# Nine units for twelve, states on the whole array and the first tap on ScalarE, in a kernel of decay attention and gated convolution

## The chip, the cores and the metric

The kernel runs on one core of a Trainium2 chip. The metric is device time in microseconds (us), as a median of runs. The five engines are TensorE (PE in the profile; PEld is its weight load), VectorE (DVE), ScalarE (ACT), GpSimd (POOL) and SyncE (SP), which here only issues transfers.

## The reference

Four batches, eight heads, 768 steps, head width 48. Each head keeps a 48x48 complex state that decays per key channel; its real part, read by the query, is the output of the step. The outputs of all heads, side by side (384 channels), go through a causal convolution of five taps whose sigmoid gates a projection, and a second projection follows.

```python
scale = np.minimum(mag, 0.999) / (mag + 1e-06)        # mag = |a|
a_re_n, a_im_n = a_re * scale, a_im * scale
for t in range(S):
    S_re, S_im = ar * S_re - ai * S_im + k[t] (x) v[t], ar * S_im + ai * S_re
    y[t] = q[t] . S_re
gate = 1 / (1 + np.exp(-sum(conv_w[k] * xp[:, k:k + S])))   # x = y of all heads, 5 taps
out = (gate * (x @ w_val)) @ w_out
```

## The kernel before

The loop over steps is turned into chunks of 128 steps. The running product of the decays is kept as a level (a log magnitude) and an angle, summed along time. Keys are divided and queries multiplied by that product (as cosine and sine, so 96 numbers for a head), after which the work of a chunk is: scores of keys against queries, a triangular mask, the masked scores against v, and the queries against the state that all earlier chunks left.

A **unit** is one tuple (batch, first head, heads, half, halves): the heads of one half (384 steps) of a batch that are prepared together. The kernel before has twelve: batch 0 is cut into 2, 2 and 4 heads for each half, the others are 8 heads wide. For each unit a chain of small steps runs on ScalarE and VectorE: logarithm, exponential, arctangent, the sums along time, two small matmuls that carry sums across partitions (`j`, `l`), sine and cosine, and at the end the scaled keys `kx` (second step of `q`) and scaled queries `qx` (second step of `r`). ScalarE reads a function from one of three table sets, and `act()` issues a table load (line 136) wherever the next function's set is not the one loaded.

From there two ways lead on. TensorE transposes `kx` and `qx` (`T`, three matmuls for a head; ScalarE copies the result out, `U`); and `kx` is stored to DRAM and read back in another layout (`K` then `N`, tiles `kd` and `kn`), because the state update needs steps on the partitions. Per chunk and group of up to two head pairs follow: scores `s`, mask `M` (VectorE), state update `t` into the one bank `S_ps` and its copy `u` (ScalarE), output `y` into `y_ps` and its copy `v` (ScalarE). Before the change `t` issues two matmuls of 64 weight columns for a head (and each is two instructions on the engine, since the data are float32); `kn` has 32 padding columns that GpSimd zeroes.

Finished outputs go by transfers on GpSimd's queue (`X`) into `xT`, 384 channels on the partitions. VectorE runs the taps of the convolution (`C`, `D`: one TENSOR_SCALAR, four SCALAR_TENSOR_TENSOR for a third of the channels), ScalarE the sigmoid (`G`), TensorE the value product (`P`, six instructions), VectorE the gating (`Z`), TensorE the output product (`O`, six), ScalarE the copy (`Q`), GpSimd the store (`W`). Four PSUM buffers named `mm` serve `j`, `l`, `T`, `P` and `O` in turn.

The order of all this is the string `ORDER`: each letter advances one stream by a step. `turn()` ties each instruction of PE, DVE and ACT to the one before it on its engine, so these three run in the order of the string. Transfers are not tied (`PIN_SP` is False).

## Time and profile before

| | before |
|---|---|
| median of 3 runs | 343.71 us (341.5 to 344.56) |
| profiled execution, first to last instruction | 343.3 us |
| PE busy | 279.2 us, 3219 matmuls |
| DVE busy | 256.9 us, 394 instructions |
| ACT busy | 252.8 us, 480 instructions |
| table loads on ACT | 34 |

The profiled execution has no other time of its own than its span, which lies 0.4 us under the median. A busy PE is not a PE at its peak, since matmuls overlap. The windows below give for a stretch of the span how long each engine was busy, how many instructions it ran, and the TensorE clock that was granted.

### The profile page before, as it was taken

The page shows a single profiled execution, that of the slowest core. Times are in us where ns is not written, and L with a number is a line of the kernel's source. Part 1 is how long each engine was busy: PE and PEld are TensorE (multiplying, and loading weights), DVE is VectorE, ACT ScalarE, POOL GpSimd, SP SyncE. Part 2 cuts the span into 40 slices and gives each one's busy share as a digit, 9 for nine tenths or more (in the row PEclk, how much of TensorE's full clock was granted, in tenths as well). Part 3 has the DMA queues.
Part 4 walks back from the last instruction along what each step waited for, and adds up shares of the span by engine and source line. Part 5 has one row for each costly group of instructions (what it writes and reads, how often), then busy time and mean ns, then how long its engine had stood idle before and what let it go on. Part 6 is the DMA issues. An engine that isn't in the chain of part 4 may idle for free.

```text
span 343.3 us, 8085 instructions
## 1 busy us (share of the span) xinstructions
PE 279.2 (81%) x3219; PEld 213.4 (62%) x3219; DVE 256.9 (75%) x394; ACT 252.8 (74%) x480; POOL 61.6 (18%) x141
## 2 busy tenths in 40 slices
...
GB/s 146 195 340 156 199 212 171 2 208 174 135 270 228 47 240 342 218 304 236 80 243 244 187 267 257 238 135 29 60 250 194 164 193 20 38 35 69 69 73 2
DMA packets 87497, 57.23 MB, mean 167 GB/s; under 512 B 43791, under 2 KB 82974, under 8 KB 86686
## 3 DMA queue, kind: packets, MB, share of 16 engines
...
q8 instruction: 27, 0.44, 0.6%
...
## 4 chain that ended last, share of the span: by engine, by line
PE 42%; ACT 14%; DVE 13%; DMA 13%; issue 11%; POOL 3%; SPq 1%; POOLq 0%; DVEq 0%; ACTq 0%
PE mm L513 10%; DMA kn<-kd 8%; PE mm L714 6%; PE y_ps L617 4%; PE sc_ps L542 4%; PE S_ps L580 4%; ACT L136 4%; PE mm L348 4%; DMA kd<-kx 3%; DVE kx L463 3%; PE mm L707 3%; PE y_ps L627 2%; PE y_ps L622 2%; ACT tmp L138 2%; ACT qx L138 2%
## 5 line engine op out<-in xcount | busy, mean ns | idle before, releaser
L676 DVE SCALAR_TENSOR_TENSOR z<-xT,cw_sb,z 128x384 f32<-128x384 f32 x96 | 55.3, 614 | 0.9
L148 POOL DMA_DIRECT2D xT<-y_sb x80 | 40.9, 517 | 77.4 <-ACT y_sb L141 69.4
L714 PE MATMUL mm<-w_sb,z 128*128 128x384 f32 x144 | 48.7, 489 | 2.7 <-DVE z L731 2.3
L707 PE MATMUL mm<-xT,w_sb 128*128 128x384 f32 x144 | 50.5, 499 | 0.0
L136 ACT ACT_TABLE_LOAD x34 | 43.6, 1283 | 1.4 <-PEq L940 0.8
L542 PE MATMUL sc_ps<-qT,kT 96*64 96x128 f32 x192 | 38.9, 300 | 3.2 <-ACT qT L141 2.5
L138 ACT ACTIVATE main<-main 128x1152 f32<-128x1152 f32 (+2 forms) x48 | 40.3, 842 | 1.4 <-DVE main L432 0.8
L558 DVE TENSOR_TENSOR sm<-sc_ps,mask 128x384 f32<-128x384 f32 (+1 forms) x54 | 27.1, 510 | 19.1 <-PE y_ps L627 11.4
L513 PE MATMUL mm<-ident,kx 128*96 128x128 f32 x192 | 30.1, 304 | 12.8 <-DVE kx L463 12.2
L714 PEld LDWEIGHTS mm<-w_sb,z 128*128 128x128 f32 x144 | 26.9, 190 | 21.2 <-DVE z L731 3.1
L543 PE MATMUL sc_ps<-qT,kT 96*64 96x128 f32 x192 | 38.9, 300 | 0.0
L707 PEld LDWEIGHTS mm<-xT,w_sb 128*128 128x128 f32 x144 | 27.2, 195 | 17.1 <-issue 0.6
L580 PE MATMUL S_ps<-v_in,kn 128*64 128x48 f32 x640 | 29.2, 236 | 5.8 <-DMA kn<-kd 4.3
L513 PEld LDWEIGHTS mm<-ident,kx 128*96 128x96 f32 x192 | 23.1, 140 | 16.3 <-issue 7.4
L141 ACT COPY qT<-mm 96x384 f32<-96x384 f32 x64 | 27.7, 485 | 6.5 <-PE mm L513 6.5
L141 ACT COPY y_sb<-y_ps 112x256 f32<-112x256 f32 (+1 forms) x54 | 18.3, 356 | 18.7 <-PE y_ps L627 18.6
L580 PEld LDWEIGHTS S_ps<-v_in,kn 128*64 128x64 f32 x640 | 25.1, 150 | 11.0 <-issue 6.6
L513 PE MATMUL mm<-ident,qx 128*96 128x128 f32 x192 | 28.6, 290 | 1.8 <-DVE qx L463 1.8
L141 ACT COPY kT<-mm 96x384 f32<-96x384 f32 x64 | 27.5, 483 | 3.3 <-PE mm L513 2.7
L141 ACT COPY ot<-mm 128x384 f32<-128x384 f32 x24 | 11.3, 472 | 23.7 <-PE mm L714 20.3
L544 PE MATMUL sc_ps<-qT,kT 96*64 96x64 f32 x192 | 28.4, 232 | 0.0
L547 PE MATMUL sc_ps<-qT,kT 96*64 96x64 f32 x192 | 28.2, 231 | 0.0
...
## 6 DMA issues: line engine op xcount, KB each, us to landing
...
```

What stands on the lines that cost most here:

```text
L136: turn("act", nc.scalar.preload_act_table_set(sets[0]))
L138: return turn("act", nc.scalar.activation(*args, **kw))
L141: return turn("act", nc.scalar.copy(out, in_))
L148: ins = (nc.gpsimd if pool else nc.sync).dma_start(**kw)
L513: pe(nc.tensor.transpose(pt[:C2, j, :], src[:, j, f, h, :], ident))
L542: pe(nc.tensor.matmul(lo[:, :C], part(u, 0, ha, n, 0, HC), part(u, 1, ha, n), start=True, stop=True))
L543: pe(nc.tensor.matmul(hi[:, 0::2], part(u, 0, hb, n, 0, HC), qb, start=True, stop=True))
L544: pe(nc.tensor.matmul(lo[:, C:], part(u, 0, hb, n, HC, C), part(u, 1, hb, n, HC, C), start=True, stop=True))
L580: pe(nc.tensor.matmul(S_ps[b][c:c + 64, head(u, h) * D:(head(u, h) + 1) * D], kn[:, at:at + 64], v_b[b][:, head(u, h), n], start=(i == fir ...
L676: dve(nc.vector.scalar_tensor_tensor(out=z, in0=xT[:, c, EXT + t0 - t:EXT + t0 - t + n], scalar=cw_sb[:, TAPS - 1 - t, c:c + 1], in1=z, op ...
L707: pe(nc.tensor.matmul(pv[:, :n], wv_sb[:, ci, c * P:(c + 1) * P], xT[:, ci, EXT + t0:EXT + t0 + n], start=(ci == 0), stop=(ci == NT - 1),))
L714: pe(nc.tensor.matmul(po[:, :DM], z[:, ci, m:m + P], wo_sb[:, ci, :], start=(ci == 0), stop=(ci == NT - 1)))
```

## The change

- **Units**: batch 0 is cut into 2 heads, 6 heads (first half) and 8 heads (second half): nine units for twelve. `groups` is made so that head pairs keep their places.
- **Tiles**: `main` (level and angle in one tile, three buffers) becomes `lv` and `an`, two buffers each; the negative exponential of `p_exp` goes into a tile `em` of its own, which shares two buffers with `tmp`.
- **Convolution**: `CONVS` runs over 768 steps at once for batches 0 to 2 and in two halves for batch 3. The first tap runs on ScalarE (`TAP0 = 'act'`).
- **States**: `t` issues one matmul with 96 weight columns for a head instead of two with 64; the padding of `kn` and its memset go, and the columns of `S_ps` are laid out so that `u` reads one run.
- **Outputs**: `y_ps` becomes one slot in a bank, instead of two slots in a bank.
- **Order**: a new string. The `pool()` helper changes nothing while `PIN_SP` is False.

```diff
-UNITS = ((0, 0, 2, 0, 1), (0, 1, 2, 0, 1), (0, 2, 4, 0, 1), (0, 0, 2, 1, 1), (0, 1, 2, 1, 1), (0, 2, 4, 1, 1), (1, 0, 8, 0, 1), (1, 0, 8, 1, 1), (2, 0, 8, 0, 1), (2, 0, 8, 1, 1), (3, 0, 8, 0, 1), (3, 0, 8, 1, 1))
+UNITS = ((0, 0, 2, 0, 1), (0, 1, 6, 0, 1), (0, 0, 8, 1, 1), (1, 0, 8, 0, 1), (1, 0, 8, 1, 1), (2, 0, 8, 0, 1), (2, 0, 8, 1, 1), (3, 0, 8, 0, 1), (3, 0, 8, 1, 1))
 PIECES = ((0, 0, 384), (0, 384, 384), (1, 0, 384), (1, 384, 384), (2, 0, 384), (2, 384, 384), (3, 0, 384), (3, 384, 384))
-CONVS = ((0, 0, 384), (0, 384, 384), (1, 0, 384), (1, 384, 384), (2, 0, 384), (2, 384, 384), (3, 0, 384), (3, 384, 384))
+CONVS = ((0, 0, 768), (1, 0, 768), (2, 0, 768), (3, 0, 384), (3, 384, 384))
 GROUPWISE = True
-BUFS = {'in': 4, 'v': 2, 'kn': 2, 'xT': 2, 'z': 3, 'main': 3, 'tmp': 1, 'qx': 2, 'kx': 1, 'kT': 6, 'S': 1, 'S_sb': 3, 'S_cr': 4, 'y_sb': 3, 'sm': 2, 'ot': 2, 'mm': 4}
-YSLOTS = 2
+BUFS = {'in': 4, 'v': 2, 'kn': 2, 'xT': 2, 'z': 2, 'lv': 2, 'an': 2, 'tmp': 2, 'qx': 2, 'kx': 1, 'kT': 6, 'S': 1, 'S_sb': 3, 'S_cr': 4, 'y_sb': 3, 'sm': 2, 'ot': 2, 'mm': 4, 'y': 1}
...
+TAP0 = 'act'
 ORDER = (
-    "AAVaaaabbcVcedhhVjfkgkciicleAmAdAnhhojoAkknLoLoLfpgipiqlAamrpqAaArTpKbTUTwcAwwTwcUeUUwwsfwwgsMMsdqry"
-    "AhivhqjNMTraTakKUbUAkcicnAewwfAlTmNTgdwUtUoshuiohijwlsmktawyapMbsukcqtctpAeyquuftvMuTKvgnrTUiTArUATU"
-    "iwUlTATUTUmtNwTyyMuXvwvyaXvawXUbUwsXcscetMdMsdhwuohwojtyuktvMyukwnyvohohvwjXkwpkpqXqpAprTKrfATUgATUA"
-    "CTUCUDnCsqsCNqoMTMoCTKCUDAsUCyDCPaMCDvaNCDbGtrPcZArdiAiAluGTmTUtZUtuhsuGthsjyckyPupevpMMvsZaXyqyvMXA"
-    "vqaykvTKfXTbTTXUUgOUUnriOcArQNcWiTlUeATQUTWATmUUfssMgstdyMiuMvtohyiuhlvojmykOvVXkpQqpXqAnWaaDTKCTDUC"
-    "TUDTUCPUDCDCoDboPDcDDdPDrhGAGZAGZZrONpcAqTQTTUWTUeATUTUTUThUTqpjsastaMKMskuyUtUTMUTbUTuTvTftktryuunt"
-    "gyuvtNUrUTUTUsuAvscXAMTAMTcsiiyXUUMlUUTmvTTteTdyuyhvohttUUjUUTkvTuTXusoktsMTMspXyUyMUqUTUTuOnCAqvvpy"
-    "OUCKUDQCvDfXsCDsQMaTMXsCUyaCDyCvNMTDvTWUCTUybUWPvVCXCgGPGGZciXPZdirlZAomOAAoDDOCQDWCDpOCDDQqpWPDcACD"
-    "tQPCuWDDGrtGPGuZTZtUZtuhTuTrUTUTUTTUhATUjqTtassaMKMsAkyUyUMUvbTuTUTvTkTtrnyNUUTUTUesuAvsXMfTMTsgyXUy"
-    "UUMUTivTvTicltcmyueUtUtUsvusXuMftMsgyydMXiTThUTUiTUhlUvTvmTUTuyoCDjUCUODvoCXDCOQDXCDCGOkGQCWskpsWMCs"
-    "nMyqpyMPQqvWvyoCKTZVTCUTUTrUPUvorXPGZTNZXTUTUOUOpDQDpWqOQDWCTDTUCTUsDUDsMDsGMyQDTWMTUDTUTqUTUtvTutyu"
-    "DKtCvtuyCuCtUrTUTGsGUsMUvsMuXrtyNuyvXTvTMUTUEyUEvTETXUTUTUTUsUsMtMXsuttuyutMvyCDyvCuDTCTUTDUTUTCTUDP"
-    "UUCDGCGCsvZXsMMsCyXCyMvCyGvPvXPZXPZOZDDODQWDDODGDQDWDPCDQCWCPCCZPGZGOZOQWOQWPQWPZZOOQWOQWQW"
+    "AaaabaLwwwwwwAbwwVAcccefgiilmceAAAdhhjdphhkkLjkkqAfgiinproAoqrKnooaalmppNwwbcdcqrTTAATqraKVthehUafuj"
+    "bktUcTTUgkceUUisMsiuslnfMdtgwoioThNyilmpUTUmAATUhqMLTTvUUTUTuUpyvTTtqUTsMyutssrTTpuMUUvryUMUtwsvyTpT"
+    "AuAaMwvabtTwssUuwcyMvjAkceAktKNyMvTUUUuryvtTfTgwqnUAAAATTiyUUssTTTXMutivoyoqusUTdtUUUlTuUUtTMTXXTXvy"
+    "rmXutMaKhThvyaUTUbUsvwMjpXkcUqyvsMcsMkUpTuUNyvTTynVUUvTTeXrXwwXUUsstwTMTTMTsXfgywooutvMyutqCvCyCDDCu"
+    "DtUUTUUATUTTTUUUsUvuwTsTPUMysTMCCdthGvuDhUPUDjGArZtyZTaMTTvyaiUUKkNUvTTiUluknssUbcmpCTTPMUyCtCswdMMu"
+    "tvTooyAqAPAuCAXUvyqGZOTcQZTteOpUTAUutTrrUTQOvhUTuUXfsgiMisaabyUUvlKsXTTcMyhmjXUcMvykNkWQXpXPPZVvetpn"
+    "oToXWqZOUTODDDDutUTUCTCutXQTCUTUsTDsUPCutMDDdsyGCUPMGZDTDWhWQDAZqhvryuvOQGPZrfWWtugAOOUjMQUaakQATUTA"
+    "yTUbUTTUTUiUvcissWlMyTkncsUTTUmMvtuKpNATMUqUyvWoPTZTTyUUAeoTTvTsMtufsyMsqKNgtivypuAitUOUTMUTUXrXTvyd"
+    "QuthUhjvTuUPUkUssMsyvMlknooWmZPZpyvOQprOQMyvVtuqTUTUTTUUtTrTTUUUTTUTTTUsMUsyTTMqrXXutvuyvtustUUUUuMX"
+    "XTTTXCXKyTUTUssUMMWvyNTsTvyMDUUUDCUtvyuTTTvCUCTTUUstUUsMWTCsMyMutTDTTCCGXDXUTvyutXUTUvyutXUUUssMsMPP"
+    "vyMPPZDvyXCOvuXCCyGZPQGZZZWODvXXCDDDPZDGDCQWDDDPDZPCOQWOQOOWQQOECCGZPCDPGDDPZCCOCCCCCCCWQOWQGWOZPQDD"
+    "GZGZOWQOOWEEWQWQQWW"
 )
...
-    groups = [[range(r, min(r + 2, g // 2)) for r in range(0, g // 2, 2)] for b, h0, g, f0, nf in units]
+    groups = [
+        [range(max(r, h0) - h0, min(r + 2, h0 + g // 2) - h0) for r in range(h0 - h0 % 2, h0 + g // 2, 2)]
+        for b, h0, g, f0, nf in units
+    ]
...
+    def bank(u, rs):
+        b, h0, g, f0, nf = units[u]
+        return b, (h0 + rs[0]) // 2 % BUFS["S"]
+
     firsts = {}
     for i, (u, n, rs) in enumerate(chunks):
-        firsts.setdefault(units[u][0], i)
+        firsts.setdefault(bank(u, rs), i)
 
...
-        flat = tl[u]["kn", f] = sb.tile([C, HN * g * C2 + 32], F32, name="kn", bufs=BUFS["kn"])
-        nc.gpsimd.memset(flat[:, HN * g * C2:], 0.0)
-        kn = flat[:, :HN * g * C2].rearrange("i (n h c) -> i n h c", n=HN, h=g)
+        flat = tl[u]["kn", f] = sb.tile([C, HN * g * C2], F32, name="kn", bufs=BUFS["kn"])
+        kn = flat.rearrange("i (n h c) -> i n h c", n=HN, h=g)
...
-    y_ps = ps.tile([P, YSLOTS * 256], F32, name="y_ps")
+    y_ps = [ps.tile([P, 512], F32, name=f"y_ps{i}") for i in range(BUFS["y"])]
     sc_ps = [ps.tile([P, 512], F32, name=f"sc_ps{i}") for i in range(2)]
-    for t in [y_ps] + sc_ps:
+    for t in y_ps + sc_ps:
         dve(nc.vector.memset(t, 0.0))
...
+    def rate(u, nm, tag):
+        b, h0, g, f0, nf = units[u]
+        tl[u][nm] = sb.tile([P, JH, nf, g * D], F32, name=nm, tag=tag, bufs=BUFS[tag])
+        return views(u, nm)
...
-        tmp = tl[u]["tmp"] = sb.tile([P, nf * g * D * JH], F32, name="tmp", bufs=BUFS["tmp"])
+        tf, tj = rate(u, "tmp", "tmp")
...
+        ef, ej = rate(u, "em", "tmp")
+        act(ef, lf, AF.Exp, scale=-0.5, accum_out=over[:, 0, u:u + 1], sets=[LE])
+        yield
+        act(lf, lf, AF.Exp, scale=0.5, accum_out=over[:, 1, u:u + 1], sets=[LE])
...
-            if i == firsts[b]:
-                S_ps[b] = ps.tile([P, 512], F32, name="S_ps", bufs=BUFS["S"])
+            if i == firsts[bank(u, rs)]:
+                S_ps[bank(u, rs)] = ps.tile([P, 512], F32, name="S_ps", bufs=BUFS["S"])
             kn = tl[u]["kn", n // HN]
             for r in rs:
-                for h in (r, r + g // 2):
-                    for c in range(0, P, 64):
-                        at = ((n % HN) * g + h) * C2 + c
-                        pe(nc.tensor.matmul(
-                            S_ps[b][c:c + 64, head(u, h) * D:(head(u, h) + 1) * D], kn[:, at:at + 64],
-                            v_b[b][:, head(u, h), n],
-                            start=(i == firsts[b] and r == rs[0] and h == r), stop=(n == NCH - 2),
-                            skip_group_check=True,
-                        ))
+                for w in range(2):
+                    h = r + w * (g // 2)
+                    at = ((n % HN) * g + h) * C2
+                    pe(nc.tensor.matmul(
+                        S_ps[bank(u, rs)][:C2, (2 * (h0 + r) + w) * D:(2 * (h0 + r) + w + 1) * D], kn[:, at:at + C2],
+                        v_b[b][:, head(u, h), n],
+                        start=(i == firsts[bank(u, rs)] and r == rs[0] and w == 0), stop=(n == NCH - 2),
+                        skip_group_check=True,
+                    ))
...
-            t = sb.tile([C2, 2, len(rs) * D], F32, name=nm, bufs=BUFS[nm])
-            act_copy(t, S_ps[b][:C2, :H * D].rearrange("c (w x) -> c w x", w=2)[
-                :, :, (h0 + rs[0]) * D:(h0 + rs[-1] + 1) * D
-            ])
+            t = sb.tile([C2, 2 * len(rs) * D], F32, name=nm, bufs=BUFS[nm])
+            act_copy(t, S_ps[bank(u, rs)][:C2, 2 * (h0 + rs[0]) * D:2 * (h0 + rs[-1] + 1) * D])
...
-        return y_ps[:, (i % YSLOTS) * 256:(i % YSLOTS + 1) * 256]
+        return y_ps[i % BUFS["y"]][:, :256]
...
-        dve(nc.vector.tensor_scalar_mul(z, x0, w0))
+        if TAP0 == "act":
+            act(z, x0, AF.Copy, scale=w0)
+        else:
+            dve(nc.vector.tensor_scalar_mul(z, x0, w0))
```

## Rows read from the trace of the kernel before

**Rows 1.** The page: span, and busy time of each engine

```profile
span 343.3 us, 8085 instructions
...
PE 279.2 (81%) x3219; PEld 213.4 (62%) x3219; DVE 256.9 (75%) x394; ACT 252.8 (74%) x480; POOL 61.6 (18%) x141
```

**Rows 2.** Windows: length; busy us of PE, PEld, DVE, ACT, POOL; clock, DMA share

```profile
0.00:140.00 140.00, 91.23 (x829) 69.47 (x830) 110.69 (x188) 117.61 (x218) 18.43 (x55) 0.90 0.75 192
140.00:333.00 193.00, 187.99 (x2392) 143.91 (x2390) 146.26 (x207) 135.21 (x263) 42.60 (x85) 1.00 0.62 156
...
60.00:70.00 10.00, 6.70 (x116) 5.92 (x112) 6.13 (x9) 6.09 (x13) 2.38 (x6) 0.81 0.05 14
70.00:80.00 10.00, 7.67 (x52) 6.27 (x54) 9.69 (x21) 9.31 (x20) 0.67 (x2) 0.53 0.78 226
110.00:120.00 10.00, 9.00 (x110) 6.85 (x110) 5.36 (x7) 5.90 (x9) 1.91 (x5) 0.83 0.24 55
```

**Rows 3.** The chain of the whole span, in order of time: start, us, what

```profile
44.98 1.21 DVE kx L463
...
49.82 0.98 PE mm L513 x9
...
52.11 5.48 DMA kn<-kd
...
105.01 5.47 DMA kn<-kd
...
237.24 5.80 PE mm L714 x18
...
267.38 2.48 DVE kx L463
...
275.79 8.10 DMA kn<-kd
```

**Rows 4.** Timeline of PE, 283 to 293 us: start, us, line, out<-in

```profile
284.31 0.29 PE L542 MATMUL sc_ps<-qT,kT 96*64 96x128 f32 x1
...
284.66 0.28 PE L542 MATMUL sc_ps<-qT,kT 96*64 96x128 f32 x1
...
285.00 1.09 PE L580 MATMUL S_ps<-v_in,kn 128*64 128x48 f32 x32
285.92 0.61 PE L617 MATMUL y_ps<-qT,S_cr 96*48 96x128 f32 x8
286.36 0.40 PE L622 MATMUL y_ps<-sm,v_in 128*48 128x64 f32 x8
286.58 0.39 PE L627 MATMUL y_ps<-sm,v_lo 128*48 128x64 f32 x8
```

**Rows 5.** Timeline of PE, 181 to 196 us

```profile
183.49 0.39 PE L627 MATMUL y_ps<-sm,v_lo 128*48 128x64 f32 x8
183.81 6.07 PE L707 MATMUL mm<-xT,w_sb 128*128 128x384 f32 x18
```

**Rows 6.** Timeline of PE, 327 to 333 us

```profile
326.62 5.65 PE L714 MATMUL mm<-w_sb,z 128*128 128x384 f32 x17
```

**Rows 7.** Groups by line and shape: count, busy us, mean ns, idle before

```profile
L676 DVE SCALAR_TENSOR_TENSOR z<-xT,cw_sb,z 128x384 f32<-128x384 f32 x96 | 55.3, 614 | 0.9
...
L136 ACT ACT_TABLE_LOAD x34 | 43.6, 1283 | 1.4 <-PEq L940 0.8
...
L138 ACT ACTIVATE main<-main 128x1152 f32<-128x1152 f32 x24 | 28.0, 1166 | 0.3
...
L138 ACT ACTIVATE z<-z 128x384 f32<-128x384 f32 x24 | 11.6, 524 | 4.6 <-DVE z L676 4.5
...
L673 DVE TENSOR_SCALAR z<-xT,cw_sb 128x384 f32<-128x384 f32 x24 | 9.7, 417 | 2.9 <-DMA xT<-y_sb 2.9
...
L461 DVE TENSOR_TENSOR main<-main,k_in 128x1152 f32<-128x1152 f32 x6 | 8.1, 1353 | 1.7 <-ACT main L138 1.7
...
L461 DVE TENSOR_TENSOR main<-main,k_in 128x288 f32<-128x288 f32 x4 | 1.8, 452 | 0.1
```

More of the change, by code (lines that the diff above doesn't have):

```diff
@@ L132, in dve, with pool @@
         return turn("dve", ins)
+    def pool(ins):
+        return turn("pool", ins) if PIN_SP else ins
     def act(*args, sets=(), **kw):
@@ L148, in dma @@
         ins = (nc.gpsimd if pool else nc.sync).dma_start(**kw)
-        return turn("sp", ins) if PIN_SP and not pool else ins
+        return turn("pool" if pool else "sp", ins) if PIN_SP else ins
     def load(u, nm):
@@ L357, in p_ln @@
     def p_ln(u):
-        b, h0, g, f0, nf = units[u]
-        tl[u]["main"] = sb.tile([P, 2, JH, nf, g * D], F32, name="main", bufs=BUFS["main"])
-        main, mf, mj = views(u)
-        act(mj[:, 0], jm(tl[u]["ar"]), AF.Ln, sets=[LE])
+        lf, lj = rate(u, "lv", "lv")
+        act(lj, jm(tl[u]["ar"]), AF.Ln, sets=[LE])
         yield
-        act(mf[:, 1], mf[:, 0], AF.Exp, scale=-1.0, accum_out=over[:, 2, u:u + 1], sets=[LE])
+        af, aj = rate(u, "an", "an")
+        act(af, lf, AF.Exp, scale=-1.0, accum_out=over[:, 2, u:u + 1], sets=[LE])
         yield
     def p_tan(u):
-        main, mf, mj = views(u)
-        dve(nc.vector.tensor_tensor(out=mj[:, 1], in0=mj[:, 1], in1=jm(tl[u]["ai"]), op=ALU.mult))
+        af, aj = views(u, "an")
+        dve(nc.vector.tensor_tensor(out=aj, in0=aj, in1=jm(tl[u]["ai"]), op=ALU.mult))
         yield
     def p_sec(u):
-        b, h0, g, f0, nf = units[u]
-        main, mf, mj = views(u)
-        tmp = tl[u]["tmp"] = sb.tile([P, nf * g * D * JH], F32, name="tmp", bufs=BUFS["tmp"])
-        act(tmp, mf[:, 1], AF.Square)
+        tf, tj = rate(u, "tmp", "tmp")
+        act(tf, views(u, "an")[0], AF.Square)
         yield
-        act(tmp, tmp, AF.Ln, bias=1.0, sets=[LE])
+        act(tf, tf, AF.Ln, bias=1.0, sets=[LE])
         yield
     def p_arc(u):
-        main, mf, mj = views(u)
-        act(mf[:, 1], mf[:, 1], AF.Arctan, sets=[TRIG, SIG])
+        af, aj = views(u, "an")
+        act(af, af, AF.Arctan, sets=[TRIG, SIG])
         yield
     def p_mag(u):
-        main, mf, mj = views(u)
+        lf, lj = views(u, "lv")
         dve(nc.vector.scalar_tensor_tensor(
-            out=mf[:, 0], in0=mf[:, 0], scalar=2.0, in1=tl[u]["tmp"], op0=ALU.mult, op1=ALU.add
+            out=lf, in0=lf, scalar=2.0, in1=views(u, "tmp")[0], op0=ALU.mult, op1=ALU.add
         ))
@@ L392, in p_inv @@
     def p_inv(u):
-        main, mf, mj = views(u)
-        act(tl[u]["tmp"], mf[:, 0], AF.Exp, bias=b_inv, scale=-0.5, sets=[LE])
+        act(views(u, "tmp")[0], views(u, "lv")[0], AF.Exp, bias=b_inv, scale=-0.5, sets=[LE])
         yield
     def p_min(u):
-        main, mf, mj = views(u)
+        lf, lj = views(u, "lv")
         dve(nc.vector.scalar_tensor_tensor(
-            out=mf[:, 0], in0=mf[:, 0], scalar=2.0 * math.log(0.999), in1=tl[u]["tmp"],
+            out=lf, in0=lf, scalar=2.0 * math.log(0.999), in1=views(u, "tmp")[0],
             op0=ALU.min, op1=ALU.subtract,
```

53 lines of the change are left out of this document (26 added, 27 removed).

## The prediction

> **What bounds the kernel now.** I read the page first: three engines are busy for three quarters of the span or more and none for all of it [rows 1]. Such shares are averages over unlike stages, so I cut the span into windows and looked for the place where the engine with no pause changes. It lies near 140 us [rows 2]. Before it ScalarE is busy for 117.6 of 140 us and VectorE for 110.7, while TensorE shows 91 us of busy time that is mostly single matmuls waiting one by one. After it TensorE is busy for 188 of 193 us at full clock, and ScalarE for 135. So the time is a sum of two stages: a front that ends when ScalarE has done 117.6 us of its own work, and a rest that lasts as long as TensorE's remaining work. The last matmul ends at 326.62 + 5.65 = 332.3 us [rows 6], and the last copy, the last store and the closing of the program take 343.3 - 332.3 = 11.0 us more.
>
> To see whether the rest is work or waiting, I priced TensorE's steps by their steady rate, from the start of one run of matmuls to the start of the next. Three transposes of a head (`T`): 9 in 0.98 us, so 0.327 us. A `P` or `O` of six: 18 in 5.80 us, so 1.935 [rows 3]. Scores of a head pair: 284.66 - 284.31 = 0.35; I take 0.34. States of a head pair, eight instructions: (285.92 - 285.00) / 4 = 0.23. Outputs of a pair: 0.44 / 2 = 0.22 for the carried part and 0.22 for the two masked parts together [rows 4]. An offset (`j`, `l`) of 8 heads is two instructions of 384 columns, 0.65. One price more: the eight masked matmuls at 183.49 should take 0.22 us, as in rows 4, but the value product behind them begins 0.32 us later [rows 5]. Going from matmuls that use part of the columns to ones that use all of them costs 0.10 us; I charge the same for the way back.
>
> The order string shows how many steps lie behind 140 us (the point is found by adding up ScalarE's steps to 117.6 us; row means over-count overlapping instructions, so they are scaled by 0.885 to give the 252.8 us of rows 1): 86 `T` (28.1 us), 72 pairs of scores (24.5), 60 of states (13.8), 72 of outputs, 60 of them with a carried part (29.0), 38 `P` and `O` (73.5), 8 offsets (5.2) and 60 changes between part and whole array (6.0). That is 180.1 us in 192.3 us: 12.2 us of waiting. The whole is **117.6 + 22.4 (ScalarE idle in the front) + 180.1 + 12.2 + 11.0 = 343.3**.
>
> **The change, part by part.** *ScalarE's own work.* Walking the new string with the rule of `act()`, the table loads fall from 34 to 25: 9 x 1.283 = 11.5 us. Three units fewer save eleven functions each; the columns stay the same, so only the fixed part goes, 1166 - 864 x 0.84 = 0.44 - 0.24 = 0.2 us a piece, about 9 us with the accumulator reads and the operands per partition. The taps add nine of 768 columns and six of 384. A sigmoid of 384 takes 0.524 us [rows 7]; with 0.84 ns for each column more and 0.1 us for the per-partition factor that is 0.95 and 0.62, together 12.2 us. Wider sigmoids and fewer copies give 2.5. Net -10.8, or -9.5 scaled: 243.3 us. *VectorE's.* The first taps leave (24 x 0.417 = 10.0), the other taps go from 96 x 0.614 = 59.0 to 24 x 0.614 + 36 x 1.014 = 51.2 (1.04 ns a column from the 1353 and 452 ns of rows 7), three units fewer give 6.5: about -23 us of 256.9. Neither total sets the end, but both fall in the stage behind the front, where they stand idle more often already.
>
> *The front.* I took the new string to the same 117.6 us of ScalarE. VectorE is at 107 us there, so it does not take over. What TensorE has done by then differs little from before: about as many flips and scores, six `P` and `O` fewer. So the front is shortened only by what ScalarE idles. Two windows hold 8.0 of its 22.4 us: 60 to 70 and 110 to 120 us, busy 6.1 and 5.9, VectorE 6.1 and 5.4 [rows 2]. The chain says why: states waited for `kn<-kd` until 57.6 and 110.5 us [rows 3]. From the end of `kx` (46.2) to that landing is 11.4 us, and the last unit's way, from 269.9 to 283.9, is 14.0. In the old string ScalarE has 10 and 11 us of own work between `kx` and the first `t` of the units concerned. In the new one it has 14 for the first unit, 22, 18, 20, 24, 19, 23 and 17 for the next seven, and 11 for the last, where TensorE has 16. The way fits in, so I take 7 of the 8 us away and leave 15.4. TensorE's clock in the window behind the first stall was 0.53 of full, the lower level of 1.2 GHz for most of it [rows 2], after a stretch with few matmuls; I count nothing for that beyond the idle time itself. At best the idle time falls to about 10, since its beginning (first loads, tables, the chain of the first unit) stays; at worst all 22.4 us remain: units of 6 and 8 heads give the in-order engines less to do beside a long step.
>
> *States on the whole array.* This is the cost of unknown size. No row shows 96 weight columns with 48 moving ones. Outputs take 0.055 us for each two part-array matmuls at 64 moving columns and 0.11 at 128: they go by the moving columns. States move only 48 and should take 0.041, yet take 0.0575: they go by their 64 weight columns, at 0.9 ns each. With 96 that is 0.083 us for one whole-array matmul, where two part-array ones of 64 ran side by side in 0.0575. A head pair (four instructions) then costs 0.33 instead of 0.23. Lower bound: the moving columns alone, 0.041, so 0.16. Upper bound: a transpose, 96 weight and 128 moving columns, 0.109, so 0.44. I take 0.33, the estimate nearest to the row of the same operands.
>
> *Changes of the array's use.* Scores and outputs still use part of the columns, so nearly each `t` now stands between two changes: the new string has 140 in all where the old has 90, and 86 behind the point where the old has 60. The rows priced each at 0.1 us. The Trainium skill, "TensorEngine Tiling (Array Packing)", section "Key Properties", says that changing the tiling mode drains TensorE, and its section "When to Use Tiling" speaks for the two 64-column halves: it speaks against this edit. It gives no time for a drain; by rows 5 it agrees, and if its speed-up of 2 for halves held here in full, a pair would go to 0.46 and the sum would be 6 us higher.
>
> *The rest.* Behind the point the new string leaves 71 `T` (23.2), 60 pairs of scores (20.4), 48 of states (15.8), 60 and 52 of outputs (24.6), 46 `P` and `O` (89.0), 6 offsets (3.9) and 86 changes (8.6): 185.5 us, 5.4 more than before. Of its waiting, 12.2 us before, I take 8: the old string has 8 places where a `t` follows a `t` with no work between, though the copy of `S_ps` must come first, the new one has none; and ScalarE and VectorE have 10 to 25 us less to do beside. *One slot for outputs* costs nothing by the string: no `y` follows a `y` directly (17 do before, filling both slots). *The memset of `kn`* waits long on GpSimd, but no store or `X` behind it had its data earlier, so 0. *Taps on ScalarE* wait for `xT` with all of ScalarE's copies queued behind; the string leaves 5 to 24 us of other work between the last `v` and its tap, more than before, so 0, at worst a few us at each of five groups. The end stays 11.0.
>
> Sum: **117.6 + 15.4 + 185.5 + 8 + 11.0 = 337.5 us** in the terms of the profiled execution, whose span lies 0.4 under the median: 338.
>
> **The rivals.** *Slower: TensorE's new work is not paid for.* If ScalarE's front idles as before and the rest waits as before, the sum is 117.6 + 22.4 + 185.5 + 12.2 + 11.0 = 348.7: states and changes cost, nothing is won. It decides once idle and waiting together pass 29 us (34.6 before). For it: the front has 14 us of idle time that I could not pin on the store and re-load of `kx`. By the page of the Trainium skill named above it would be 6 us more. Chance 0.20, together with a milder form in which `X` lands late and the first tap stops ScalarE.
> *No change*: 26 to 32 us of idle and waiting, 340 to 347 us. For it: a stall removed often reappears one step later. Chance 0.24.
> *Much faster: the whole-array states go by their moving columns.* Then the rest is 185.5 - 48 x 0.17 = 177.3, the sum 329, with idle time at its best 325. Against it: the states of before, which go by their weights. Chance 0.14.
> That the edits do not act can be ruled out for the computing engines, which run the string; the transfers are free of it, and if loads go out late the front's idle time grows, inside the first rival.
>
> **How the numbers follow.** The forecast, 331 to 340 us, has 0.42. A measurement of this kernel tells about 1%, 3.4 us, from no change. Faster by more (under 340.3): 0.42 + 0.14 = 0.56. Within it: 0.24. Slower: 0.20. For 8 in 10 the range goes from the quick states (327) to the slow rival (349): 327 to 350.
>
> **What would show it.** In the new profile: 25 table loads; ScalarE reaching 117.6 us of busy time near 133 us, and no stretch of 10 us before it in which ScalarE and VectorE both fall to 6; states in runs at 0.083 us from start to start; TensorE dense from there to about 326 us. Wrong would be: ScalarE or TensorE idle behind `kn<-kd` again, first taps that wait for `xT<-y_sb`, or states at 0.04 or 0.11 us.

## The result, and where the time came from

The changed kernel takes **327.5 us** (median of 4 runs, 326.6 to 328.4) where the kernel before takes 344.1 (341.5 to 346.2): 0.952 of it, with an interval of 0.947 to 0.957. The direction was forecast, the size was not: 338 us was predicted, 6 us faster, and it is 16 to 17. Single executions now and then run about 2% longer than the others, and the medians below leave them out. The page of the changed kernel, in answer to [rows 1]:

```profile
span 325.9 us, 7175 instructions
...
PE 279.0 (86%) x2887; PEld 209.5 (64%) x2887; DVE 240.1 (74%) x289; ACT 241.3 (74%) x430; POOL 59.6 (18%) x129
```

ScalarE's total is 2 us under the forecast (243.3) and VectorE's 6 us over it (about 234), so less work explains little of the miss. The windows, cut as in [rows 2], show where it is:

```profile
0.00:124.00 124.00, 89.24 (x1062) 70.82 (x1063) 113.29 (x135) 117.73 (x201) 20.64 (x53) 1.00 1.05 252
124.00:315.00 191.00, 189.78 (x1828) 138.72 (x1826) 126.76 (x155) 123.52 (x230) 38.40 (x76) 1.00 0.53 134
60.00:70.00 10.00, 9.32 (x144) 8.09 (x140) 9.87 (x13) 10.00 (x21) 2.71 (x6) 1.00 0.93 244
70.00:80.00 10.00, 9.85 (x144) 8.69 (x143) 9.88 (x10) 9.97 (x19) 2.47 (x5) 1.00 1.21 245
110.00:120.00 10.00, 10.00 (x110) 7.59 (x110) 9.08 (x11) 9.93 (x15) 2.29 (x5) 1.00 1.07 221
```

ScalarE has done the 117.6 us of work by which I marked the end of the front at 123.9 us, not at 140; it idles 6.3 us of them, where before it idled 22.4. The last matmul ends at 314.6 us:

```profile
308.54 5.97 PE L726 MATMUL mm<-w_sb,z 128*128 128x384 f32 x18
314.43 0.19 PE L507 MATMUL mm<-ones,hits 128*1 128x1 f32 x2
```

With TensorE's matmuls behind 123.9 us priced as in the prediction (183.5 us of own work in 190.7), the sum of the run stands beside the forecast's:

| term, us | before | forecast | run |
|---|---|---|---|
| ScalarE's own work in the front | 117.6 | 117.6 | 117.6 |
| ScalarE idle in the front | 22.4 | 15.4 | **6.3** |
| TensorE's own work behind it | 180.1 | 185.5 | 183.5 |
| its waiting | 12.2 | 8 | 7.2 |
| end | 11.0 | 11.0 | 11.3 |
| span | 343.3 | 337.5 | 325.9 |

Of the 11.6 us between forecast and run, 9.1 are one term: the front's idle time. These are the front's stretches, first before, then after (length, then PE, PEld, DVE, ACT, POOL busy, clock, DMA):

```profile
0.00:10.00 10.00, 0.00 (x0) 0.00 (x0) 5.49 (x9) 6.18 (x12) 5.11 (x23) 1.00 0.73 157
10.00:60.00 50.00, 30.80 (x279) 25.48 (x281) 38.74 (x83) 42.80 (x93) 2.95 (x8) 0.97 0.85 212
60.00:80.00 20.00, 14.37 (x168) 12.19 (x166) 15.82 (x29) 15.40 (x33) 3.06 (x7) 0.67 0.42 120
80.00:110.00 30.00, 25.12 (x242) 17.33 (x238) 26.31 (x38) 28.01 (x48) 3.87 (x9) 0.99 0.72 205
110.00:130.00 20.00, 14.47 (x129) 11.07 (x130) 14.81 (x21) 15.32 (x23) 3.33 (x7) 0.74 0.73 159
```

```profile
0.00:10.00 10.00, 0.25 (x1) 0.17 (x1) 7.10 (x13) 6.01 (x11) 5.01 (x21) 1.00 0.81 194
10.00:60.00 50.00, 27.61 (x195) 18.95 (x197) 43.98 (x55) 49.47 (x78) 0.00 (x0) 1.00 1.02 270
60.00:80.00 20.00, 19.17 (x286) 16.78 (x282) 19.75 (x22) 19.97 (x39) 5.18 (x11) 1.00 1.07 244
80.00:110.00 30.00, 28.20 (x421) 24.02 (x421) 29.38 (x32) 28.34 (x55) 5.81 (x12) 1.00 1.12 260
110.00:130.00 20.00, 20.00 (x235) 15.43 (x235) 19.05 (x23) 19.90 (x32) 4.76 (x10) 1.00 1.16 217
```

Length less ACT is ScalarE's idle time. The first 10 us keep theirs (3.8 and 4.0), and nearly so do 80 to 110 us (2.0 and 1.7). From 10 to 60 us it falls from 7.2 to 0.5, from 60 to 80 from 4.6 to 0, from 110 to 130 from 4.7 to 0.1. The prediction had a reason for a window in each of the last two of these (60 to 70 and 110 to 120 us) and took 10 to 60 us for fixed. The clock is full in all of after's rows, 0.67 and 0.74 in two of before's.

### The profile page after: what moved, and what is told of

Its sections match the earlier page's. It is cut to its first block, busy times and chain, and to the rows that moved or that the text cites. A ratio compares the mean times of both kernels' runs of the same rounds, so it can differ in the third digit from the quotient of the medians.

```text
span 325.9 us, 7175 instructions
## 1 busy us (share of the span) xinstructions
PE 279.0 (86%) x2887; PEld 209.5 (64%) x2887; DVE 240.1 (74%) x289; ACT 241.3 (74%) x430; POOL 59.6 (18%) x129
## 3 DMA queue, kind: packets, MB, share of 16 engines
q1 hardware_dynamic: 80142, 47.21, 59.8%
## 4 chain that ended last, share of the span: by engine, by line
PE 51%; ACT 17%; issue 11%; DMA 9%; DVE 4%; POOL 3%; SPq 1%; POOLq 0%; ACTq 0%
PE mm L719 10%; PE mm L524 8%; PE mm L726 7%; PE S_ps L591 6%; PE y_ps L626 5%; PE sc_ps L553 5%; DMA v_lo<-in_v_dram 4%; ACT tmp L147 4%; PE mm L361 2%; PE y_ps L636 2%; PE y_ps L631 2%; ACT lv L147 2%; ACT kT L150 2%; POOL out_dram L157 2%; PE sc_ps L555 2%
## 5 line engine op out<-in xcount | busy, mean ns | idle before, releaser
L688 DVE SCALAR_TENSOR_TENSOR z<-xT,cw_sb,z 128x768 f32<-128x768 f32 (+1 forms) x60 | 50.2, 854 | 5.2 <-ACT z L147 4.3
L726 PE MATMUL mm<-w_sb,z 128*128 128x384 f32 x144 | 49.6, 491 | 0.0
L591 PE MATMUL S_ps<-v_in,kn 128*96 128x48 f32 x320 | 35.6, 252 | 7.4 <-DMA kn<-kd 6.2
L591 PEld LDWEIGHTS S_ps<-v_in,kn 128*96 128x96 f32 x320 | 32.4, 168 | 13.4 <-DMA kn<-kd 6.0
L553 PE MATMUL sc_ps<-qT,kT 96*64 96x128 f32 x192 | 36.6, 287 | 0.6 <-DVE sm L569 0.6
L554 PE MATMUL sc_ps<-qT,kT 96*64 96x128 f32 x192 | 36.7, 287 | 0.5 <-ACT qT L150 0.5
L719 PEld LDWEIGHTS mm<-xT,w_sb 128*128 128x128 f32 x144 | 26.4, 190 | 16.6
L157 POOL DMA_DIRECT2D out_dram<-ot x24 | 13.2, 550 | 104.4 <-ACT ot L150 86.8
L150 ACT COPY kT<-mm 96x384 f32<-96x384 f32 x64 | 28.6, 486 | 0.5 <-PE sc_ps L558 0.2
L555 PE MATMUL sc_ps<-qT,kT 96*64 96x64 f32 x192 | 27.3, 224 | 0.0
L558 PE MATMUL sc_ps<-qT,kT 96*64 96x64 f32 x192 | 27.1, 223 | 0.0
L743 DVE TENSOR_TENSOR z<-mm,z 128x384 f32<-128x384 f32 x24 | 13.0, 554 | 15.6 <-ACT z L147 9.4
```

The costliest lines, as they stand in the source:

```text
L150: return turn("act", nc.scalar.copy(out, in_))
L157: ins = (nc.gpsimd if pool else nc.sync).dma_start(**kw)
L553: pe(nc.tensor.matmul(lo[:, :C], part(u, 0, ha, n, 0, HC), part(u, 1, ha, n), start=True, stop=True))
L554: pe(nc.tensor.matmul(hi[:, 0::2], part(u, 0, hb, n, 0, HC), qb, start=True, stop=True))
L555: pe(nc.tensor.matmul(lo[:, C:], part(u, 0, hb, n, HC, C), part(u, 1, hb, n, HC, C), start=True, stop=True))
L558: pe(nc.tensor.matmul(hi[:, 1], part(u, 0, ha, n, HC, C), part(u, 1, ha, n, HC, C), start=True, stop=True))
```

## The experiments

Ratios are to the kernel before, with 95% intervals. "Idle" is ScalarE's idle time until it has 117.6 us of work behind it.

### The states, part of the array or the whole

**States in halves again, in the kernel after.**

```diff
-                    at = ((n % HN) * g + h) * C2
...
+                    for c in range(0, P, 64):
+                        at = ((n % HN) * g + h) * C2 + c
...
+                            kn[:, at:at + 64], v_b[b][:, head(u, h), n],
```

> The kernel after, its states back in two matmuls of 64 weight columns for a head. Theory A (the kernel after is bound by ScalarE up to 124 us and by TensorE's own work from there; a head pair's states cost 0.33 us on the whole array and 0.23 in halves; the changes between part and whole array stay, since in the new string the steps beside a t are as often T, P or O as s or y): the 48 pairs behind 124 us give 4.8 us back, so 327.5 goes to about 322.5 us, 0.937 of the kernel before. Rival B (halves are worth a factor of two, as the prediction's sentence on the skill had it): about 317 us. Rival C (TensorE has slack, states are not on the path): 327 us, unchanged. In the trace A has S_ps pairs at 0.23 us and TensorE's last matmul near 310 us.

Measured: 324.7 us, 0.944 (0.936 to 0.952), the best of all versions; its four runs (323.9 to 325.2) lie under all runs of the kernel after. TensorE's own work, priced as before, falls by 7.0 us in all (80 head pairs at 0.10, less ten changes of use more) and by 4.8 behind 124 us; the last matmul ends 3.4 us earlier, at 311.2. So the whole array costs, B and C are out, and A has the cause and somewhat too large a size (2.8 us for 4.8).

**Whole-array states in the kernel before**, the same edit the other way.

> The kernel before with one matmul of 96 weight columns for a head's states instead of two of 64, all else as it was. The old string has 60 head pairs behind its 140-us point and 10 changes of the array's use more. Theory A (0.10 us more for a pair and 0.10 us for a change, TensorE the bound there): 344 + 6 + 1 = 351 us, 1.02 of the kernel before. Rival B (a whole-array state costs no more, since it issues half the instructions): 344 us. Rival C (halves are worth a factor of two): 358 us.

Measured: 353.8 us, 1.033 (1.026 to 1.040); the profiled span grows by 6.7 us, to 350.0. A, with the median 3 us above the 351 expected. In the trace of the kernel after, states, transposes and scores follow each other so (start, us, line, instruction):

```profile
160.28 0.80 PE L591 MATMUL S_ps<-v_in,kn 128*96 128x48 f32 x8
160.91 0.82 PE L524 MATMUL mm<-ident,qx 128*96 128x128 f32 x6
161.57 0.80 PE L591 MATMUL S_ps<-v_in,kn 128*96 128x48 f32 x8
162.21 0.82 PE L524 MATMUL mm<-ident,kx 128*96 128x128 f32 x6
162.96 0.32 PE L553 MATMUL sc_ps<-qT,kT 96*64 96x128 f32 x1
```

Eight instructions of states take 0.63 to 0.64 us up to the start of the next step; but for the first two, one starts every 0.085 us, where I estimated 0.083. The price of a change of use stands in these rows too: six transposes take 0.66 us up to the next states (160.91 to 161.57), which use the whole array as they do, and 0.75 us up to scores (162.21 to 162.96), which use part of it. That is 0.09 us, where I charged 0.10.

**Fewer changes of the array's use**: 24 letters `t`, `s`, `y` of the string moved a few places, 102 changes for 150 (the expectation counts one less of each).

```diff
-afujbktUcTTUgkceUUisMsiuslnfMdtgwoio
+afutjbkUcTTUgkceUUisMsiustlnfMdgwoio
```

> The kernel after with states in halves, and 24 of the t, s and y letters moved a few places in the order, past steps of TensorE that do not depend on them, so that they stand beside others that use part of the array: 101 changes of the array's use for 149 (57 for 87 behind 124 us). Theory A (a change costs TensorE 0.1 us): 3 us less than with states in halves alone, about 321 to 322 us. Rival B (a change costs nothing when other matmuls are queued): 324.7 us. Rival C (later t and y hold back the copies behind them): slower than 325 us.

Measured: 334.0 us (331.9 to 336.4), 0.975 (0.966 to 0.984): C. What the changes left out should save (48 by 0.1 us) is more than lost: in the trace, of the fastest execution, idle rises from 6.5 to 9.6 us, and outputs wait for the copy out of their one slot. TensorE's longest group of waits (us in total, times, longest), 1.2 us with states in halves alone:

```profile
PE y_ps L628 <- ACT y_sb L150: 5.2, 8, 1.3
```

On the price of a change itself the run's time says nothing.

### The edits outside the order

**First tap on VectorE again** (`TAP0 = 'dve'`).

> The kernel after with the first tap of the convolution back on VectorE. Theory A (ScalarE and VectorE set the end only in the front, where three of the fifteen first taps lie; behind it TensorE does): 327 us, within 2 of the kernel after. Rival B (VectorE, busy over 9.5 of 10 us in most of the front, is as much the bound as ScalarE): 1 to 3 us slower, about 330. Rival C (the taps on ScalarE hold back its copies while they wait for xT): 2 to 4 us faster, about 324.

**Two output slots again.**

```diff
-        return y_ps[i % BUFS["y"]][:, :256]
+        return y_ps[0][:, (i % 2) * 256:(i % 2 + 1) * 256]
```

> The kernel after with two output slots in the one bank, as before. Theory A (no output directly follows an output, so one slot is always free in time): 327.5 us, within 1. Rival B (outputs wait for the copy out of the one slot): 2 to 3 us faster, about 325. Rival C (a copy reading the bank while TensorE writes its other half holds either back): slower than the kernel after by 1 us or more.

**Each tap of 768 as two of 384.**

```diff
+        for s in parts:
+            ... z[:, s] ...
```

> The kernel after with each 768-wide tap issued as two of 384, in the same order. It adds 36 instructions on VectorE at some 0.2 us of fixed cost (7 us) and 9 on ScalarE (3 us). Theory A (VectorE's total does not set the end): 327 to 329 us. Rival B (VectorE is near the bound from 40 to 130 us and pays for it): 330 to 335 us.

**These three and the states in halves together.**

> The kernel after with its four edits outside the order undone: states in halves, first tap on VectorE, two output slots, taps of 384. What stays is the nine units, their tiles and the new string. Theory A (units and order make the whole gain, the whole-array states take 5 us of it back, the rest is worth nothing): 322 to 325 us. Rival B (wide taps and the tap on ScalarE carry part of the gain): 330 to 337 us.

Measured: tap 329.3 us, 0.957 (0.947 to 0.966); slots 327.7, 0.953 (0.945 to 0.961); narrow taps 327.3, 0.953 (0.943 to 0.962); all together 327.2, 0.954 (0.948 to 0.960). Slots and tap width are worth nothing. The tap is worth some 2 us, the size of rival B; its cause is shown in part. With the tap on VectorE, idle rises by 4.1 us to 10.4. Of this 1.3 lie between 110 and 120 us, where VectorE has no pause and ScalarE has:

```profile
110.00:120.00 10.00, 10.00 (x110) 7.57 (x111) 10.00 (x13) 8.60 (x12) 3.03 (x6) 1.00 1.09 232
```

The other 2.9 lie between 100 and 110 us. There VectorE is busy for 8.1 of 10 us, more than two taps of 0.94 us have left ScalarE, and it waits 3.3 us for outputs of TensorE (1.1 in the kernel after), which itself stood still for 1.1 us at 96.5 in the one execution traced. In the run of all four edits together VectorE has no pause from 110 to 130 us (20.00 of 20) and ScalarE idles 3.1 us there.

The last run gives up 2 us with the tap and wins 2.8 with the states, and falls between the two ranges expected. **Nine units, their tiles and the new string make the gain; the other four edits cancel.**

### The store and re-load of the keys

**No way over DRAM, in the old and in the new string.**

```diff
-        kd = tl[u]["kd"][(f - f0) * HS:(f - f0 + 1) * HS]
+        kd = k[b].rearrange("h s d -> (h s d)")[:HS * g * C2].rearrange("(s h c) -> s h c", h=g, c=C2)
```

and each `N` of the string moved to stand right before its `K`.

> The kernel before, with kn read from the input k laid out as kd is, instead of from the stored kx, and issued ahead of that store: the states do not wait for the way over DRAM. It leaves out that the state is made of the scaled keys; transfers, sizes and work stay. Theory A, the prediction's (the two windows where ScalarE and VectorE both fall to 6 are this wait, 8 of the 22.4 us that ScalarE idles in the front): 336 us. Rival B (the wait makes nearly all of the idle time behind 40 us, by late copies and a slower TensorE clock behind it): 330 us or less, ScalarE's idle time in the front under 10 us. Rival C (the stall moves one step on): 342 to 344 us.

> The kernel after with kn read from the input k, laid out as kd is and issued ahead of the store of kx (the state is not made of the scaled keys). Theory A (in the new string other work covers the way of kx over DRAM for every unit but the first, whose wait lies on TensorE while ScalarE is the bound): 326 to 328 us, unchanged. Rival B (the way still costs behind some units): 320 to 324 us.

Measured: in the old string 338.0 us, 0.985 (0.978 to 0.992), idle 17.9; in the new one 326.7, 0.952 (0.946 to 0.957), against 327.5. So the new string does cover the way, and in the old one it cost 6 us. But only one of my two windows was this wait. The old string without it:

```profile
60.00:80.00 20.00, 13.51 (x160) 11.09 (x159) 16.31 (x31) 15.19 (x31) 2.95 (x7) 0.82 0.46 134
110.00:130.00 20.00, 14.93 (x72) 9.19 (x66) 17.75 (x24) 18.20 (x24) 3.30 (x7) 0.83 0.92 248
```

From 110 to 130 us ScalarE idles 1.8 us where it idled 4.7. From 60 to 80 us it idles 4.8, as before.

**Is it TensorE's clock?** Matmuls that nothing reads, ahead of the steps at which TensorE stands still for 1 to 5 us.

```diff
+    filler = {203: 10, 237: 8, 288: 40, 356: 12, 493: 40, 535: 18, 541: 9}
     for at, key in enumerate(ORDER):
+        if at in filler:
+            spare = mm()
+            for _ in range(filler[at]):
+                pe(nc.tensor.matmul(spare[:, :P], ident, ident, start=True, stop=True))
         next(streams[key])
```

> The kernel before with 137 idle matmuls (128x128, into a spare tile that nothing reads) put in front of seven steps at which TensorE stands still for 1 to 5 us between 48 and 139 us, so many that they fit in the pause. Data, order and waits of the work stay. Theory A (TensorE's lower clock, granted from 57 to 64, 71 to 81, 112 to 115 and 122 to 129 us, is what stretches the chain of copies and outputs at 60 to 70 us): the clock stays at full level in most of 57 to 129 us, ScalarE idles 2 to 4 us less, time 339 to 342 us. Rival B (the lower clock only accompanies the pauses): clock up, time 344 us. Rival C (the pauses are too scattered, the clock falls as before): no change in either.

> The kernel before with kn read from the input k ahead of the store (as in the run without the way over DRAM, which took 338 us with ScalarE idle for 17.9 us in the front) and with the same 137 idle matmuls. Theory A (way and lower clock together make the idle time from 57 to 129 us, the rest is the beginning, 10 us up to 60 us): ScalarE idles 13 to 15 us in the front, 334 to 336 us. Rival B (what is left at 60 to 70 us is the order of the steps alone): 338 us, idle time unchanged.

Measured: 351.0 us, 1.018 (1.011 to 1.025), and 345.6, 1.005: slower by 7 than without filler, although the clock was full in the front, but for 3.4 us in the first. These two decide nothing: one such matmul is two instructions, 0.11 us apart each, so the filler was twice as long as the pauses and stood in the way. With 60 instead of 137:

> As the kernel before without the way over DRAM and with idle matmuls, but with 60 instead of 137 of them: each turned out to be two instructions of 0.11 us, so the first form (345.6 us) put 9 us of filler into pauses of 5. Theory A (the lower TensorE clock at 57 to 64 and 71 to 74 us stretches the old string's chain at 60 to 80 us): full clock there, ScalarE's idle time in the front falls from 17.9 to 14 to 16 us, the time from 338 to 335 us. Rival B (the order of the steps makes that idle time): full clock, 338 us, idle time 17 to 18 us.

Measured: 337.4 us, 0.978 (0.970 to 0.986), idle 18.2, with

```profile
60.00:80.00 20.00, 15.75 (x207) 13.71 (x202) 18.00 (x36) 16.38 (x34) 3.02 (x7) 0.89 0.47 134
110.00:130.00 20.00, 18.09 (x136) 13.59 (x130) 17.74 (x24) 18.26 (x25) 3.45 (x8) 1.00 0.90 245
```

The clock goes from 0.82 and 0.83 to 0.89 and 1.00. ScalarE's busy time from 60 to 80 us grows by 1.2 us, from 110 to 130 us it stays at 18.2, and neither the idle time of the whole front nor the time moves by more than 0.7 us: rival B. The pause itself, without the filler and with it:

```profile
60.00:70.00 10.00, 5.89 (x100) 5.33 (x99) 6.50 (x11) 5.86 (x13) 2.95 (x7) 0.80 0.21 53
```

```profile
60.00:70.00 10.00, 8.94 (x152) 8.46 (x146) 8.19 (x15) 7.14 (x17) 3.02 (x7) 1.00 0.22 53
```

At full clock 2.9 of its 4.1 us of idle time are left, so the lower clock may have had 1.3 us of it; from 10 to 60 us ScalarE idles 0.8 us more than without filler. Another stretch shows two clocks without any filler: from 30 to 50 us the clock was full in the kernel before, and at the lower level for most of the time in the run without the way over DRAM (before, then that run):

```profile
30.00:50.00 20.00, 15.73 (x140) 13.35 (x137) 18.63 (x39) 17.29 (x41) 0.12 (x1) 1.00 0.79 187
```

```profile
30.00:50.00 20.00, 15.55 (x135) 13.10 (x132) 18.63 (x39) 17.38 (x41) 0.12 (x1) 0.58 0.82 193
```

ScalarE idles 2.7 us in the one and 2.6 in the other. So the lower clock accompanied the old string's pauses and, but for a microsecond or so, did not make them.

### The beginning of the front

What did ScalarE wait for from 10 to 60 us before? Its waits there: what, for whom, us in total, times, longest.

```profile
ACT qT L141 <- PE mm L513: 1.4, 1, 1.4
ACT qx L138 <- DVE main L424: 1.2, 1, 1.2
ACT y_sb L141 <- PE y_ps L627: 0.8, 3, 0.5
ACT main L138 <- DVE main L432: 0.8, 1, 0.8
ACT S_sb L141 <- PE S_ps L580: 0.7, 1, 0.7
```

Round trips through VectorE and TensorE, 0.5 to 1.4 us at the longest, and none of these waits is itself one for a load (the last, at 59.8 us, stands behind `kn<-kd`). In the kernel after ScalarE's timeline (end of the line: idle time before it) is closed up: functions of units 2 and 3, 1152 columns wide, stand between the copies of units 0 and 1:

```profile
35.26 0.46 ACT L150 COPY kT<-mm 96x384 f32<-96x384 f32 x1
35.62 1.16 ACT L147 ACTIVATE an<-lv 128x1152 f32<-128x1152 f32 x1
...
36.77 1.24 ACT L147 ACTIVATE tmp<-lv,b_inv 128x1152 f32<-128x1152 f32 x1
...
38.41 1.17 ACT L147 ACTIVATE tmp<-an 128x1152 f32<-128x1152 f32 x1
39.48 0.47 ACT L150 COPY qT<-mm 96x384 f32<-96x384 f32 x1
39.84 1.17 ACT L147 ACTIVATE tmp<-tmp 128x1152 f32<-128x1152 f32 x1
```

**Unit 3 later**: six letters of it, four on ScalarE and two on VectorE, move behind the first flips and copies; no work is added.

```diff
-ATqraKVthehUafujbktUcTTUgkceUUisMsiuslnfMdtg
+ATqrKVthehUfujktUTTUgkUUisMsiuslnaabccefMdtg
```

> The kernel after with six letters of unit 3 (both steps of a, b, both of c, e: logarithm, exponential, tangent product, square, logarithm, sum) held back by up to 35 places in the order, behind the first flips and copies of units 0 and 1. Nothing is added; table loads stay at 25. Theory A (the front lasts as long as ScalarE's own work plus what it idles, and it is the early work on later units that fills the round trips of the first ones): ScalarE idles 4 to 7 us more before 60 us, and the time grows by as much, to 331 to 335 us. Rival B (other work takes the place, or the idle time is won back later): 327 to 329 us.

Measured: 345.5 us, 1.004 (1.001 to 1.008). The whole gain is gone. Idle is 21.3 us, and the same place shows why:

```profile
35.38 1.26 ACT L147 ACTIVATE tmp<-lv,b_inv 128x1152 f32<-128x1152 f32 x1 [1.06 <-DVE lv L397]
...
38.81 0.47 ACT L150 COPY qT<-mm 96x384 f32<-96x384 f32 x1 [1.30 <-PE mm L524]
...
45.86 1.16 ACT L147 ACTIVATE tmp<-an 128x1152 f32<-128x1152 f32 x1 [1.42 <-DVE an L380]
```

From 30 to 50 us ScalarE idles 6.4 us where it idled 0.3, within the 4 to 7 of A. But 8 us more fall between 110 and 130 us, and they were not expected:

```profile
109.52 0.45 PE L636 MATMUL y_ps<-sm,v_lo 128*48 128x64 f32 x2 [2.29 <-DMA v_lo<-in_v_dram]
112.75 0.66 PE L636 MATMUL y_ps<-sm,v_lo 128*48 128x64 f32 x6 [2.79 <-DMA v_lo<-in_v_dram]
```

`v_lo` is one tile for all batches. It is loaded again when the last output of batch 0 has read it, and the first outputs of batch 1 wait for that. To take this wait out, GpSimd copies `v_lo` from `v_in`:

```diff
-            dma("V", out=v_lo[w * HC:(w + 1) * HC, hs]..., in_=v[b, hs]...)
+            lo = slice(w * HC, (w + 1) * HC)
+            pool(nc.gpsimd.tensor_copy(out=v_lo[lo, hs], in_=v_b[b][lo, hs]))
```

> The run with unit 3's steps held back (345.5 us; ScalarE idles 21.3 us in the front), with v_lo filled by GpSimd from v_in instead of by transfers. Theory A (two costs: 6 us of bare round trips at 30 to 50 us, and a late batch 0 whose reload of v_lo then stops TensorE at 107 to 113 us): ScalarE's idle time falls to 12 to 15 us, the time to 333 to 338 us. Rival B (the second stall has another cause): idle time 19 us or more, 342 us or more.

Measured: 337.4 us, 0.983 (0.977 to 0.989), idle 13.2: A. The second stall cost 8 us. The other 10 over the kernel after are the bare round trips, 6.9 of them as idle time; copying `v_lo` may be in the rest, since it cost the best version 1.5 us (below).

**Eleven units in the new order**: units 1 and 2 cut in two, the two halves one behind the other at each step; then with `v_lo` copied too.

```diff
-UNITS = ((0, 0, 2, 0, 1), (0, 1, 6, 0, 1), (0, 0, 8, 1, 1), ...
+UNITS = ((0, 0, 2, 0, 1), (0, 1, 2, 0, 1), (0, 2, 4, 0, 1), (0, 0, 4, 1, 1), (0, 2, 4, 1, 1), ...
+SETS = ((0,), (1, 2), (3, 4), (5,), (6,), (7,), (8,), (9,), (10,))
...
-        for u in range(NU):
-            yield from gen(u)
+        for us in SETS:
+            for _ in zip(*[gen(u) for u in us]):
+                yield
```

> The kernel after in its own order, but with units 1 and 2 cut again into two each (2 and 4 heads, 4 and 4 heads); the two halves of a unit go through each step one behind the other, so order, head pairs, TensorE's steps and table loads stay. It adds 22 ScalarE functions at 0.24 us with six reads of accumulators at 0.1, about 6 us, and as much on VectorE, nearly all ahead of 124 us. Theory A (the front lasts as long as ScalarE's own work plus the 4 us of the start, so narrow units are paid in full, and the order, not the width, keeps ScalarE from idling): ScalarE idles 6 us in the front as in the kernel after, the time is 331 to 334 us. Rival B (wide units are what covers the round trips): ScalarE idles 10 us or more, 336 us or more. Rival C (the front does not set the time): 328 us.

> The run with eleven units (333.9 us; ScalarE idles 10.3 us in the front, 6.3 of them at 100 to 110), with v_lo filled by GpSimd from v_in instead of by transfers. Theory A (of the 6.4 us over the kernel after, 4 are the later v_lo and 2.7 ScalarE's own longer work): ScalarE idles 5 to 7 us, the time is 329 to 331 us. Rival B (the stall at 100 us has another cause): 333 us or more.

Measured: 333.9 us, 0.968 (0.961 to 0.975), idle 10.3; with `v_lo` copied 332.7, 0.971 (0.963 to 0.978), idle 8.0. The time of the first fits A, its idle time is rival B's: 6.3 us of it lie at 100 to 110 us. The wait there was not the one for `v_lo` that the second run's theory took it for:

```profile
102.84 1.17 PE L602 MATMUL S_ps<-v_in,kn 128*96 128x48 f32 x6 [3.81 <-DMA v_in<-in_v_dram]
```

TensorE stood still for `v_in`. With `v_lo` copied this wait is gone and 3.4 us of idle time are left there, 1.6 of them ScalarE's for `xT` ahead of a first tap. So copying takes 2.9 us of that idle time away but only 1 us of the time; 332.7 lies between A's range and rival B's 333. What speaks for A in the first run is the beginning: with operations as narrow as these ScalarE still idles 0.2 us from 10 to 60. The order fills it, not the width. Two units more cost 5 to 6 us: 2.9 of ScalarE's total (244.2), 1.7 of idle time (8.0 for 6.3), the rest not traced.

**The best version with `v_lo` copied.**

> The kernel after with states in halves (324.7 us), and v_lo filled by GpSimd from v_in, which holds the same rows on the same partitions, instead of by two transfers for a unit; in the chain of waits of the kernel after these transfers stand twice, with 6.6 and 7.1 us. Theory A (the transfers are on the path where an output waits for v_lo, 1.1 us of visible wait): 1 to 2 us faster, 323 us. Rival B (the chain only passes through them beside other work): 324.7 us. Rival C (GpSimd now waits for the last output of a batch with the collecting transfers queued behind): slower than 326 us.

Measured: 326.2 us, 0.946 (0.940 to 0.952), 1.5 us slower than the best. B or C; nothing is won where the transfers have time.

In one table, ScalarE's idle time in the front and the end of TensorE (us; worked out from the traces):

| kernel | idle | ScalarE's total | last matmul ends | median |
|---|---|---|---|---|
| before | 22.4 | 252.8 | 332.3 | 344.1 |
| before, no way over DRAM | 17.9 | 252.4 | 325.3 | 338.0 |
| after, unit 3 later | 21.3 | 242.9 | 330.8 | 345.5 |
| the same, v_lo copied | 13.2 | 242.4 | 323.7 | 337.4 |
| after, eleven units | 10.3 | 244.0 | 320.6 | 333.9 |
| after | 6.3 | 241.3 | 314.6 | 327.5 |
| after, states in halves | 6.5 | 241.1 | 311.2 | 324.7 |

Holding unit 3 back adds 15.0 us of idle time and 16.2 us to the end of TensorE: the front's idle time is paid in full, since behind it TensorE has no slack.

## Why the prediction was off

**The step that failed** is "take 7 of the 8 us away and leave 15.4", with its floor, "at best the idle time falls to about 10, since its beginning (first loads, tables, the chain of the first unit) stays". The beginning that stays is 4.0 us. The 7.2 us from 10 to 60 us were round trips of small units with too little other work between, and the new string puts work there; holding six letters of it back brought 6.2 us of idle time back there. I had that in hand: the string shows unit 3's steps between the flips of units 0 and 1. I had read the idle time only in the two windows where it was densest, and declared the rest fixed without asking what ended it.

**The reason given for the 8 us was half right.** The wait for `kn<-kd` made the window at 110 us (4.7 us of idle time from 110 to 130 fell to 1.8 without it), not the one at 60 us, which stayed. The chain showed `kn<-kd` ahead of both [rows 3], but a piece of a chain ahead of a pause is not its cause. That the new string covers the way was right: removing it there changes 0.8 us, and the one long wait of after, 5.5 us of `S_ps` for `kn` early on, is TensorE's while ScalarE is busy.

**The clock**: counting nothing for it beyond the idle time was right to about 1 us, as the run with 60 idle matmuls and the stretch from 30 to 50 us show.

**The states** were sized well: 0.085 us from start to start for the 0.083 estimated, and giving them up wins 2.8 us of the 4.8. The fast rival with moving columns alone is out; the time it forecast, 325 to 329, was met for another reason. The Trainium skill, "TensorEngine Tiling (Array Packing)", section "When to Use Tiling", gives a twofold column tiling where the weight columns are 64, as each half has them. The run with halves agrees that they are faster, at the size of the rows (0.23 for 0.33 us a pair) and not at a factor of two, by which rival B of that run had 317 us.

**Changes of use** were priced rightly: 0.09 us in the rows for 0.10. (The old string has 88 of them, not 90; the 60 behind the point are right.) TensorE took 190.7 us behind the front for the 193.5 forecast. But putting states in halves does not lower their number in this string (150 for 140), and lowering it by hand cost 9 us.

**The taps on ScalarE** were taken as 0, "at worst a few us". They are worth 2: I checked what ScalarE would wait for, not that VectorE, busy for 9.7 of 10 us from 60 to 130 us, would be relieved. VectorE's total fell by 17 us for the 23 forecast: the taps fell by 15 for 18, the rest by 2 for 6.5. One slot and the wide taps at 0 were right.

**What was to show it**: 25 table loads, as forecast; no stretch with both engines at 6; TensorE dense to the end, but to 315 for 326; ScalarE's 117.6 us at 124 for 133. The groups by line and shape (count, busy us, mean ns, idle before) for the prices:

```profile
L591 PE MATMUL S_ps<-v_in,kn 128*96 128x48 f32 x320 | 35.6, 252 | 7.4 <-DMA kn<-kd 6.2 <-ACT S_sb L150 1.1
L688 DVE SCALAR_TENSOR_TENSOR z<-xT,cw_sb,z 128x768 f32<-128x768 f32 x36 | 35.6, 1013 | 2.6 <-ACT z L147 2.2
...
L145 ACT ACT_TABLE_LOAD x25 | 32.1, 1283 | 1.2 <-PEq L952 0.8
...
L147 ACT ACTIVATE z<-xT,cw_sb 128x768 f32<-128x768 f32 x9 | 8.5, 943 | 0.3 <-DMA xT<-y_sb 0.3
```

Wide taps took 1013 ns on VectorE for 1014 forecast and 943 ns on ScalarE for 950. The first taps wait for `xT` for 0.3 us in all: that rival did not come either.

**Open**: what makes the old string's pause at 60 to 80 us. It was shown not to be the way over DRAM, nor, but for a microsecond or so, the clock; that it is the order of its steps is argued, not shown. The new tiles (`lv`, `an`, `em` for `main`) were never taken apart from the new string, and nine units were set in it beside eleven, not beside twelve.
